# Moving SBUF tiles to other addresses: weights at 0 and moving tiles at 64 modulo 256 bytes, in an attention, FFT and feed-forward kernel

## The chip, the core and the metric

The kernel runs on one core of a Trainium2 chip. The metric is the device time of one execution in microseconds. The profile of one execution names the engines PE (TensorE's matmuls), PEld (TensorE's weight loads), DVE (VectorE), ACT (ScalarE), POOL (GpSimd) and SP (SyncE, which issues most DMAs). A matmul has two operands in SBUF: the stationary one, which a weight load brings into the array, and the moving one, which is streamed past it.

## What is computed

Cut from the reference: four batches, 12 heads, 448 tokens, head size 64, so 768 features; the feed-forward layer is 3072 wide.

```python
scores = cap * np.tanh(scale * np.matmul(q, k.transpose(0, 1, 3, 2)) / cap)
attn = np.exp(scores - np.max(scores, axis=-1, keepdims=True))
attn = attn / (np.sum(attn, axis=-1, keepdims=True) + 1e-09)
x = np.matmul(attn, v)                       # then to (batch, token, 768)
u = x + np.real(np.fft.fft(np.fft.fft(x, axis=1), axis=2))
un = (u - mean(u)) / np.sqrt(var(u) + 1e-06)
out = u + np.maximum(un @ w_ch1, 0.0) @ w_ch2
```

## The kernel before

The work has two stages that overlap a little. In the **attention stage** (to about 195 us) 84 steps run: `scores` (L398) multiplies k tiles (stationary) with q tiles (moving) in fp32, ACT takes tanh (L408) and exp (L411) into tiles `a`, and `weigh` (L427) multiplies `a` (stationary) with `vt` (moving, 65 columns). Batch by batch the FFT follows as small matmuls with constant tables (L499, L527), and the residual stream is transposed (L611).

The **feed-forward stage** (from about 200 us to the end) is in 12 rounds `g`, each of 256 of the 3072 hidden features. `up` (L737 to L758) makes, for one batch, two PSUM tiles `ph` of 18 matmuls each: six feature blocks `dc`, and for each three products, low weights with high x, high weights with low x, high with high (L744), since every fp32 number is split in two fp32r parts. Relu goes to `hh` (ACT L756 the high part, DVE L757 the low part). `down` (L760 to L792) makes six PSUM tiles `po` of 6 matmuls each, two `hh` tiles by the same three products, and DVE adds each to the residual `xc` (L787). Every matmul of both lines has 128 rows and 448 moving columns of 4 bytes, except the last group of all, which is cut into 256 and 192 columns. One round is `U0 U1 D0 U2 D1 U3 D2 D3` (L796; U is up, D is down, the digit is the batch): 36 matmuls for each letter, 288 in a round. In round 0 the order is `U0 D0 U1 D1 U2 D2 U3 D3`.

The weights come as 64-bit numbers in `raw` tiles by DMA (two buffers of tag `raw` for the first rounds, two of tag `seq` later) and are split into two fp32r parts by six or seven DVE instructions and two of ACT for each half tile (`jobs`, L634 to L695); in the feed-forward stage DVE does this for the next round while PE works on this one. The order of all steps is a written table (`ORDER`) and a fixed interleaving after it; nothing in it depends on addresses.

SBUF is handed out by `new()` (L299): all tiles of the stages come from one pool, under a tag with a number of buffers; a pool lays out its tags one behind the other. A tile of more than 100 elements is rounded up to `LINE` = 16 elements (64 bytes). Several kinds of tiles share a tag one after the other. The weights of round `g` for `up` are in tag `w1` when g is even and in tag `x0` when g is odd (`PLACE1`, L75); those for `down` take `w2a`, `w2b` and two `raw` buffers in turn (`PLACE2`, L76). The moving x operands `xs` of batch 0, 1, 2, 3 are in tags listed in `XPLACE` (L84): batches 0 and 1 in tiles that all begin at 64 modulo 256 bytes, batch 3 in `ff`, `y` and `feat`, of which five of six begin at 0. `hh` shares the five `a` buffers (L755).

Of the kernel before, what the change touches and what calls it, by code (L numbers as in the profile page):

```python
# [11 lines left out]
F32 = mybir.dt.float32  # L12
# [7 lines left out]
P = 128  # L20
# [38 lines left out]
GF = 2  # L59


LINE = 16


HI_MIN = float(np.uint32(0x38100000).view(np.float32))
# [209 lines left out]
def attention_fft_ffn(  # L275
# [12 lines left out]
    nc = tc.nc  # L288
    add, sub, mul = ALU.add, ALU.subtract, ALU.mult
    keep = ctx.enter_context(tc.tile_pool(name="keep", bufs=1))  # L290
    dram = ctx.enter_context(tc.tile_pool(name="dram", bufs=4, space=bass.MemoryType.DRAM))


    pool = ctx.enter_context(tc.tile_pool(name="pool", bufs=1))
    psum = ctx.enter_context(tc.tile_pool(name="psum", bufs=2, space=PSUM))
    stage = {}
    turn = {}

    def new(shape, dtype, tag, bufs, name):  # L299
        n = math.prod(shape[1:])  # L300
        flat = pool.tile([P, -(-n // LINE) * LINE if n > 100 else n], dtype, tag=tag, bufs=bufs, name=name)
        axes = [f"d{i}" for i in range(len(shape) - 1)]
        sizes = {a: z for a, z in zip(axes[1:], shape[2:])}
        return flat[: shape[0], :n].rearrange(f"p ({' '.join(axes)}) -> p {' '.join(axes)}", **sizes)

    def turns(shape, dtype, tags, bufs, name):
        turn[name] = n = turn.get(name, -1) + 1
        return new(shape, dtype, tags[n % len(tags)], bufs, name)
# [10 lines left out]
    ident = keep.tile([P, P], F32, name="ident")  # L319
    make_identity(nc, ident)  # L320
    capt, tscale, ncap, guard = (keep.tile([P, 1], F32, name=n) for n in ("capt", "tscale", "ncap", "guard"))
    mhalf = keep.tile([P, LINE], F32, name="mhalf")
    nc.vector.memset(mhalf, -0.5)
    nc.scalar.activation(guard, mhalf[:, :1], AF.Tanh)

# [3 lines left out]


    vt = new([P, 2, NC, D + 1], F32, "vt", 1, "vt")
    nc.gpsimd.memset(vt[:, :, :, D:], 1.0)

# [23 lines left out]
    def load_constant(i):  # L357
        n, p = divmod(i, 2)
        if p == 0:
            featT[n] = new([P, 2, S], F32, "feat", 2, "featT")  # L360
            nc.sync.dma_start(featT[n][:, :, :NJ], feat[n])
        else:
            seqT[n] = new([P, 2, NK], F32, "seq", 2, "seqT")
            nc.sync.dma_start(seqT[n], seq[n])
# [93 lines left out]
    t_t, f_t, y_t, u_t, d_t, stat, line, lnrow, rowt = ({} for _ in range(9))  # L458
# [553 lines left out]
```

## Time and profile before

| | us |
|---|---|
| median of the runs | 922.57 |
| quickest run | 922.36 |
| the profiled execution, its own time | 923.11 |
| its span, first to last instruction | 921.3 |
| PE busy in it | 908.7 |
| DVE busy | 716.6 |
| ACT busy | 327.9 |

The span is 1.8 us shorter than the execution's own time. PE's busy time counts a matmul from its start to a modelled end; the matmuls overlap, so the pace, from one start to the next, is to be taken from long stretches of equal instructions and not from the mean duration of one. The chain of waits lists, in order of time, what each stretch of the execution waited for; a row "14.40 PE ph L745 x72" is 72 matmuls in a row which took 14.40 us together.

### The profile page before, as it was taken

To read this page: it belongs to the slowest core of one execution; us is meant where nothing else is said; L and a number is where in the kernel's file an instruction comes from. 1 tells how busy PE (TensorE), PEld (TensorE's weight loads), DVE (VectorE), ACT (ScalarE), POOL (GpSimd) and SP (SyncE) were. 2 spreads that over 40 slices of the span, in tenths; PEclk is the share of its full clock that TensorE was granted. 3 is DMA by queue.
4 is the path that set the end of the run, shared out by engine and by line. 5 is a ranking of instruction groups with operands and counts; after the bars stand their busy time and mean duration, and the time that the engine had idled before them with its cause. 6 is when DMAs were issued, how large, how long until landed. Compare 5 with 4: busy or idle time off the path is not lost.

```text
span 921.3 us, 18681 instructions
## 1 busy us (share of the span) xinstructions
PE 908.7 (99%) x7836; PEld 790.8 (86%) x7836; DVE 716.6 (78%) x1467; ACT 327.9 (36%) x503; POOL 6.8 (1%) x15
## 2 busy tenths in 40 slices
PE   8999999999999999999999999999999999999998
PEld 5676766677889999999999999999999999999997
DVE  2688797999988787887878778787787877877633
ACT  7998889962412222122121222212222221222200
POOL 0000000000000000000000000000000000000000
PEclk9999999999999999999999999999999999999999
DMA  6654433400202221211212111111211112121033
GB/s 184 185 169 129 117 91 96 123 15 2 80 20 67 56 75 52 62 52 52 64 53 71 58 51 52 52 52 54 67 52 52 52 51 54 55 64 52 18 120 120
DMA packets 50612, 66.64 MB, mean 72 GB/s; under 512 B 25568, under 2 KB 36704, under 8 KB 50528
## 3 DMA queue, kind: packets, MB, share of 16 engines
q1 hardware_dynamic: 50240, 65.12, 24.7%
q8 instruction: 62, 1.02, 0.5%
q10 hardware_dynamic: 288, 0.33, 0.1%
q14 instruction: 22, 0.18, 0.1%
HBM read 59.91 MB, written 5.52 MB: 71 GB/s over the span
## 4 chain that ended last, share of the span: by engine, by line
PE 92%; DVE 3%; ACT 3%; issue 1%; DMA 1%; POOL 0%; SPq 0%; DVEq 0%; POOLq 0%; ACTq 0%
PE po L779 38%; PE ph L745 37%; PE av L427 7%; PE s L398 6%; PE pq L527 1%; PE yps L499 1%; ACT a L408 1%; ACT a L411 1%; PE pt L611 1%; DMA capt<-cap 1%; DVE u L551 0%; ACT u L602 0%; ACT hh L756 0%; DVE u L547 0%; DVE u L604 0%
## 5 line engine op out<-in xcount | busy, mean ns | idle before, releaser
L779 PE MATMUL po<-hh,w 128*128 128x448 f32 x1734 | 361.4, 366 | 1.7 <-DVE xc L787 1.3
L745 PE MATMUL ph<-xs,w 128*128 128x448 f32 x1728 | 356.5, 365 | 0.0
L779 PEld LDWEIGHTS po<-hh,w 128*128 128x128 f32 x1734 | 323.2, 188 | 32.7 <-DVE xc L787 4.7
L745 PEld LDWEIGHTS ph<-xs,w 128*128 128x128 f32 x1728 | 324.0, 188 | 25.6 <-issue 0.3
L787 DVE TENSOR_TENSOR xc<-xc,po 128x448 f32<-128x448 f32 x289 | 176.3, 615 | 41.4 <-PE po L779 41.1
L757 DVE SCALAR_TENSOR_TENSOR hh<-ph,hh 128x448 fp32r<-128x448 f32 x96 | 59.9, 624 | 95.8 <-ACT hh L756 95.6
L658 ACT ACTIVATE wt<-raw 128x384 f32<-128x384 f32 x84 | 46.5, 554 | 230.4 <-DVE w L692 230.4
L756 ACT ACTIVATE hh<-ph 128x448 fp32r<-128x448 f32 x96 | 52.4, 545 | 189.6 <-PE ph L745 189.6
L427 PEld LDWEIGHTS av<-vt,a 128*49 128x49 f32 (+3 forms) x3072 | 85.1, 130 | 28.4 <-issue 14.6
L427 PE MATMUL av<-vt,a 128*49 128x65 f32 (+3 forms) x3072 | 91.2, 222 | 1.5 <-issue 1.0
L408 ACT ACTIVATE a<-s,tscale 128x900 f32<-128x900 f32 x84 | 82.7, 1009 | 13.0 <-PE s L398 8.5
L411 ACT ACTIVATE a<-a,capt 128x900 f32<-128x900 f32 x84 | 85.7, 1047 | 0.9
L312 ACT CAST w<-wt 128x384 fp32r<-128x384 f32 x84 | 42.8, 509 | 117.7 <-DVE wt L667 117.7
L398 PE MATMUL s<-q,k 64*64 64x450 f32 x672 | 76.4, 552 | 1.8 <-ACT a L408 1.7
L667 DVE SCALAR_TENSOR_TENSOR wt<-wt 128x384 f32<-128x384 f32 x96 | 53.6, 558 | 9.6 <-DVE wt L664 0.5
L664 DVE SCALAR_TENSOR_TENSOR wt<-raw,wt 128x384 uint32<-128x384 uint32 x96 | 53.6, 559 | 3.3
L692 DVE TENSOR_TENSOR w<-wt 128x384 fp32r<-128x384 f32 x96 | 53.6, 558 | 3.3
L686 DVE SCALAR_TENSOR_TENSOR wt<-raw,wt 128x384 f32<-128x384 uint32 x96 | 53.5, 558 | 2.9
L317 DVE TENSOR_TENSOR wt<-wt,w 128x384 f32<-128x384 f32 x96 | 52.8, 550 | 0.0
L398 PEld LDWEIGHTS s<-q,k 64*64 64x64 f32 x672 | 19.9, 132 | 21.8 <-ACT a L408 10.3
L661 DVE TENSOR_SCALAR wt<-raw 128x384 uint32<-128x384 uint32 x96 | 34.1, 355 | 1.1
L683 DVE TENSOR_SCALAR wt<-wt 128x384 uint32<-128x384 uint32 x96 | 34.0, 354 | 0.6
(59 smaller groups left out, 326.1 us busy)
## 6 DMA issues: line engine op xcount, KB each, us to landing
raw<-w2r SPq DMA_DIRECT2D x48, 384.0 KB, 3.1
raw<-w1r SPq DMA_DIRECT2D x48, 384.0 KB, 3.1
q<-qr SPq DMA_DIRECT2D x35, 225.0 KB, 3.3
outT<-xc SPq DMA_DIRECT2D x23, 224.0 KB, 1.9
k<-kr SPq DMA_DIRECT2D x12, 256.0 KB, 3.2
vt<-vr SPq DMA_DIRECT2D x24, 128.0 KB, 4.3
vt<-vr SPq DMA_DIRECT2D x24, 96.0 KB, 2.5
k<-kr SPq DMA_DIRECT2D x12, 192.0 KB, 3.4
```

Source lines behind the costliest of these rows:

```text
L398: nc.tensor.matmul(ps_t[t][h * D : (h + 1) * D, n, :SQ], kt[q, k][rows, k0, h], qk[q, x][rows], start=True, stop=True,)
L408: nc.scalar.activation(a_t[t], ps_t.pop(t)[:, :, :SQ], AF.Tanh, scale=tscale)
L411: nc.scalar.activation(a_t[t], a_t[t], AF.Exp, scale=capt)
L427: nc.tensor.matmul(pa_t[p][q0:q1, j, g * (D + 1) : (g + 1) * (D + 1)], a_t[t][rows, n, OFF[g] + q0 : OFF[g] + q1], vt[rows, p % 2, i], sta ...
L664: nc.vector.scalar_tensor_tensor(tu, hi.bitcast(U32), 0xC0000000, tu, op0=ALU.bitwise_and, op1=ALU.bitwise_or)
L667: nc.vector.scalar_tensor_tensor(t, w, HI_MIN, t, op0=ALU.is_ge, op1=mul)
L686: nc.vector.scalar_tensor_tensor(w, lo, 2.0**-52, w, op0=mul, op1=mul)
L692: nc.vector.tensor_tensor(ws[c][1][:, sl], t, w, op=add)
L745: nc.tensor.matmul(ph[:, :S], w_[:, dc * P : (dc + 1) * P], x_, start=(k_ == 0), stop=(k_ == 3 * NDC - 1),)
L757: nc.vector.scalar_tensor_tensor(hh[:, 1], ph[:, :S], 0.0, f32(hh[:, 0]), op0=ALU.max, op1=sub)
L779: nc.tensor.matmul(po[:, q0:q1], w_[:, dc * P : (dc + 1) * P], hh[:, x_, q0:q1], start=(k_ == 0), stop=(k_ == 3 * GF - 1),)
L787: nc.vector.tensor_tensor(ac[:, q0:q1], ac[:, q0:q1], po[:, q0:q1], op=add)
```

## The change

The one pool is cut into three: small tiles first, then a pool of everything that is loaded as weights of the feed-forward stage and what shares its tags, then all other large tiles. Two pad tiles shift where the second and third pool begin, and `LINE` goes from 16 to 64 elements (256 bytes), so that every tile in a pool begins at the same place modulo 256 bytes. The room for it comes from small tiles that are no longer rounded up and from a descriptor scratch of 1 KB in place of 16 KB a partition, which shifts all of SBUF down.

```diff
-LINE = 16
+LINE = 64
+WEIGHTS = "w1", "x0", "w2a", "w2b", "raw", "seq", "tmp"
+SMALL = "den", "stat", "bs", "ln", "nt", "var", "rowt", "yh"
+PAD = 16, 16
...
-    pool = ctx.enter_context(tc.tile_pool(name="pool", bufs=1))
+    pools = {2: ctx.enter_context(tc.tile_pool(name="small", bufs=1))}
+    pad = ctx.enter_context(tc.tile_pool(name="pad", bufs=1))
+    pad.tile([P, PAD[0]], F32, name="pad")
+    pools[1] = ctx.enter_context(tc.tile_pool(name="weights", bufs=1))
+    gap = ctx.enter_context(tc.tile_pool(name="gap", bufs=1))
+    gap.tile([P, PAD[1]], F32, name="gap")
+    pools[0] = ctx.enter_context(tc.tile_pool(name="pool", bufs=1))
...
-        flat = pool.tile([P, -(-n // LINE) * LINE if n > 100 else n], dtype, tag=tag, bufs=bufs, name=name)
+        home = pools[1 if tag in WEIGHTS else 2 if tag in SMALL else 0]
+        size = n if tag in SMALL else -(-n // LINE) * LINE
+        flat = home.tile([P, size], dtype, tag=tag, bufs=bufs, name=name)
...
-    mhalf = keep.tile([P, LINE], F32, name="mhalf")
+    mhalf = keep.tile([P, 4], F32, name="mhalf")
...
-    nc = bacc.Bacc("TRN2", target_bir_lowering=False, num_devices=1)
+    nc = bacc.Bacc("TRN2", target_bir_lowering=False, num_devices=1, dynamic_dma_scratch_size=1024)
```

Every engine's list of instructions, with their shapes and the semaphores they wait for, is the same in both built programs, but for one memset of `mhalf` that is 4 columns wide in place of 16. What differs is addresses. The built programs give each operand's first byte in its partition; modulo 256 it is:

| operand | before | after |
|---|---|---|
| `up` weights, even g / odd g | 0 / 192 | 0 / 0 |
| `up` moving `xs`, batches 0 and 1 | 64 | 64 |
| `up` moving `xs`, batch 2 | 0, 64, 128, 192 | 64 |
| `up` moving `xs`, batch 3 | 0 (15 of 18 matmuls), 64 (3) | 64 |
| `down` weights | 192 (1155 matmuls), 0 (579) | 0 |
| `down` moving `hh`, by buffer | 128, 192, 0, 64, 128 | 64 |
| `scores` moving q, by buffer / stationary k | 128, 192, 0, 64 / 128 | 64 / 64 |
| `weigh` tile `a` by buffer / `vt` | 128, 192, 0, 64, 128 / 64 | 64 / 64 |

An offset inside a weight tile (512 bytes for a block `dc`, 3072 from the high to the low part) and from the high to the low half of a moving tile (1792 bytes) is a whole number of 256 bytes, so it changes nothing in this table. Of the 3462 matmuls of `up` and `down`, those with moving minus weights equal to 64 modulo 256 are 792 of 1728 and 330 of 1734 before, and all of them after.

## Rows read from the trace of the kernel before

**Rows 1.** The page: busy time of the engines, and the chain that ended last

```profile
PE 908.7 (99%) x7836; PEld 790.8 (86%) x7836; DVE 716.6 (78%) x1467; ACT 327.9 (36%) x503; POOL 6.8 (1%) x15
...
PE po L779 38%; PE ph L745 37%; PE av L427 7%; PE s L398 6%; PE pq L527 1%; PE yps L499 1%; ACT a L408 1%; ACT a L411 1%; PE pt L611 1%; DMA capt<-cap 1%; DVE u L551 0%; ACT u L602 0%; ACT hh L756 0%; DVE u L547 0%; DVE u L604 0%
```

**Rows 2.** Busy time by stretch: PE, PEld, DVE, ACT, POOL, then PEclk, DMA share, GB/s

```profile
300.00:350.00 50.00, 50.00 (x249) 46.51 (x248) 39.73 (x78) 11.15 (x22) 0.00 (x0) 1.00 0.21 59
```

**Rows 3.** The page's costliest groups: the two matmul lines

```profile
L779 PE MATMUL po<-hh,w 128*128 128x448 f32 x1734 | 361.4, 366 | 1.7 <-DVE xc L787 1.3
L745 PE MATMUL ph<-xs,w 128*128 128x448 f32 x1728 | 356.5, 365 | 0.0
```

**Rows 4.** Chain of waits, U0 and U1 of g=1, 2 and 4: start, us, what

```profile
274.17 14.69 PE ph L745 x72
...
332.57 14.40 PE ph L745 x72
...
449.94 14.41 PE ph L745 x72
```

**Rows 5.** Chain of waits, U3 of g=1, 2 and 8

```profile
310.68 7.24 PE ph L745 x36
...
369.16 7.29 PE ph L745 x36
...
720.79 7.39 PE ph L745 x36
```

**Rows 6.** Chain of waits, the whole round g=10 and the start of g=11

```profile
801.17 14.40 PE ph L745 x72
815.57 7.31 PE po L779 x36
822.88 7.36 PE ph L745 x36
830.23 7.32 PE po L779 x36
837.55 7.29 PE ph L745 x36
844.84 14.65 PE po L779 x72
859.49 14.69 PE ph L745 x72
```

**Rows 7.** Chain of waits: D1 of g=2, D2 with D3 of g=4, D0 of g=8

```profile
361.60 7.56 PE po L779 x36
...
493.88 14.93 PE po L779 x72
...
698.87 7.27 PE po L779 x36
```

**Rows 8.** Chain of waits, around the start of the last unbroken stretch of PE

```profile
268.46 0.54 DVE xc L787
...
269.05 5.12 PE po L779 x24
```

**Rows 9.** Chain of waits, its end

```profile
918.07 0.02 issue
```

**Rows 10.** Waits of PEld from 265 us on: total us, times, longest

```profile
PEld po L779 <- DVE xc L787: 2.8, 9, 0.5
```

**Rows 11.** Timeline of PE in the attention stage: start, us, and what

```profile
29.99 1.89 PE L398 MATMUL s<-q,k 64*64 64x450 f32 x16
31.70 2.18 PE L427 MATMUL av<-vt,a 64*64 64x65 f32 x80
...
36.27 1.74 PE L398 MATMUL s<-q,k 64*64 64x450 f32 x16
...
103.16 2.55 PE L427 MATMUL av<-vt,a 128*64 128x65 f32 x80
```

**Rows 12.** A DVE line that reads `raw` tiles: duration ns min/median/max

```profile
L664 DVE SCALAR_TENSOR_TENSOR wt<-raw,wt x96: 557/559/561, 10.5 to 865.9; 128x384 uint32<-128x384 uint32 x96
```

## The prediction

> **What bounds the kernel now.** I read the page first: PE is busy for 908.7 us of the span, and its two feed-forward lines hold 38% and 37% of the chain that ended last, the attention lines 7% and 6% [rows 1]. So what counts is how fast PE gets through its matmuls. [...]
>
> The groups by line cannot show the pace, since their matmuls overlap: 365 and 366 ns is the mean length of one, and both lines have the same form, 128x448 [rows 3]. The chain in order of time can, because it merges unbroken rows of equal matmuls. There the reader is to see two things.
>
> First, the pace is not constant although the work is. U0 and U1 of each round are 72 matmuls of one form on the same x tiles (all at 64 modulo 256). They took 14.69 us in g=1, 14.40 in g=2, 14.41 in g=4 [rows 4]. The eleven rounds after the first alternate strictly: six odd ones took 14.68 or 14.69 us, five even ones 14.40 or 14.41. What alternates with them is one thing, the place of the `up` weights: 192 modulo 256 when g is odd, 0 when it is even. That is 204.0 against 200.1 ns a matmul.
>
> Second, it is the distance between the operands that counts, not the weights' place by itself. Batch 3 has nearly all its x tiles at 0, and there the order turns round: U3 took 7.24 us in g=1, with the weights at 192, and 7.29 and 7.39 in g=2 and 8, with the weights at 0 [rows 5]. The good cases are 64 minus 0 and 0 minus 192, both 64 modulo 256; the worse ones are 128 and 0. So while a matmul streams its moving operand and the next weights are loaded, the two reads seem to hinder each other by an amount that their relative place sets. The trace shows the effect, not its mechanism.
>
> Of the whole stretch from 269.05 us, where the chain leaves DVE [rows 8], to 918.07 us [rows 9] the chain is PE without a break: 649.02 us. In it lie 24 matmuls of round 0 and eleven rounds of 288 (the last six, cut in two, count as six), 3192 in all: 203.3 ns each.
>
> **The change part by part.** *Up.* After the change all 1728 matmuls of `up` have the operands of the 14.40 us rows, 64 and 0. 936 of them have another distance now. *Down.* All 1734 of `down` get the same; 1404 have another distance now. Before, weights, `hh` tiles or both change place in the middle of each group of six, and one kind of `down` row is at distance 64 in both halves, but at different places (64 and 0, then 0 and 192): D0 of g=8, 7.27 us for 36 [rows 7], 201.9 ns. The clean round g=10 shows where `down` stands otherwise: 7.31, 7.32 and 14.65 us for 36, 36 and 72 [rows 6], 203.1 to 203.5 ns. After, nothing changes place within a group or from one group to the next, as within U0 and U1 of an even round, and the form and the sequence of low and high parts are the same. So I carry 200.1 ns over from `up`, and keep 201.9 as the other bound.
>
> The sum: at 14.405 us for 72 a matmul takes 200.1 ns, 3192 take 638.7 us, and 649.02 - 638.7 is 10.3 us. Not all of this is pace. In g=2 to 5 PE also waits: D1 took 7.56 us in g=2 [rows 7] against 7.32 in the clean round, 0.24 more, and so in four rounds, 1.0 us; D2 with D3 took up to 14.93 us [rows 7] against 14.65, about 0.6 us over the four. These 1.6 us are waits of the weight load for DVE's addition to the residual, which frees the PSUM tile [rows 10], and no address changes them. That leaves 8.7 us.
>
> Two corrections. Before 269 us the chain runs through DVE and ACT between short pieces of PE [rows 8]: this transition, with the last batch's FFT, sets its own time. Round 0 has 264 matmuls there; at 3.2 ns each (203.3 - 200.1) they could give 0.8 us, and nothing if all is hidden. I take 0.3, since most of that stretch is the other engines'. Then a faster PE meets the four waiting rounds earlier, where DVE is late already, and part of the gain turns into longer waits. If DVE alone set those four rounds, all the gain of the pace in them would be lost: a clean round is 58.32 us from start to start [rows 6] and 288 times 200.1 ns is 57.63, so 0.7 us a round, 2.8 us in four. If DVE follows, nothing is lost. DVE has 10 of 50 us free there [rows 2] and its additions follow PE's groups, so I stay near nothing and take 0.5 of the 0 to 2.8 us. Sum: 8.7 + 0.3 - 0.5 = **8.5 us**.
>
> *Attention.* Its operands move too: q and k come to the same place (64 and 64), `a` and `vt` as well. Before, q goes round four buffers at all four places and `a` round five, so a strong effect would show as steps of several lengths in turn. They don't: of the six unbroken pairs of steps in the two stretches that I read, one took 1.89 us and the rest 1.74 or a little less [rows 11]. A run of 80 `weigh` matmuls took 2.18 or 2.55 us [rows 11], which goes with its shapes. So I price the stage at nothing. If the share of long pairs went from one in six to none, 42 pairs would gain 0.025 us each, 1.0 us; if it went to one in two, they would lose 0.05 each, 2.1 us.
>
> *DVE, ACT, DMA.* Nothing is added or moved in any queue: no instruction, no wait. A DVE line that reads `raw` tiles at 192 early and at 0 later took 557 to 561 ns throughout [rows 12], so I see no price of an address there. The wider rows make no operand longer. The memset of 4 in place of 16 columns stands before the first matmul and costs nothing.
>
> The profiled execution took 923.11 us, its span 921.3; less 8.5 it would be 914.6. The median of the runs is 0.54 lower, and so is the forecast: 922.57 - 8.5 = **914.1 us**, 0.9% faster. By about 2% a measurement of this kernel tells a change from none, so this counts as the same.
>
> [...] The even and odd rows above differ by 0.28 us with nothing but an address changed [rows 4]. [...]
>
> **The rivals.** *Addresses make no difference*, and the alternation has another cause that also goes by odd and even rounds, such as which weights DVE and the DMAs write meanwhile. Then the time stays at 922.6 us. Against it stands that U3 turns the other way from U0 and U1 in the same rounds [rows 4, 5]; for it, that U3's order rests on 0.05 to 0.15 us. That the tiles don't lie where the change says is no rival: the built program gives 64 and 0 for every matmul of both lines.
>
> *Only `up` gains.* In `down` each group of six begins with a new PSUM tile, whose release and whose `hh` PE may have to wait for, and it might not settle in the quick pattern. Then the gain is `up`'s alone: in g=10 14.40 + 7.36 + 7.29 [rows 6] against 144 times 200.1 ns, 28.81, so 0.24 us; in an odd round 0.28 from the first two batches and 0.04 each from the others at 7.24; about 0.3 in eleven rounds, 3.3 us: 919.3 us. For it speaks that `down` is slower than `up` in mixed rounds. *`Down` gains in part*, as its own row at distance 64 would have it: 1.8 ns more for the 1596 matmuls of `down` in the stretch, 2.9 us, and 917.0 us.
>
> *DVE takes it back.* The four waiting rounds keep their length, and 2.8 us are lost in place of 0.5: 922.6 - 6.2 is 916.4 us. For it speaks that PE's waits in them are all for DVE [rows 10], against it that they sum to 2.8 us in nine waits, so DVE is late by little.
>
> *Attention slows* and the kernel ends slower than before. Its stationary and moving operands now begin at the same place, distance 0, which in U3 is the worse case. If all pieces went from the quick to the slow row, scores would cost 84 times 0.075 us (half of 1.89 - 1.74), 6.3 us, and `weigh` 3072 times 4.6 ns ((2.55 - 2.18) / 80), 14.2 us [rows 11]. The pieces are mixed now, so I take half, 10.3 us: 922.6 - 8.5 + 10.3 = 924.4 us. It ends slower from 8.5 us on, 4.4% of the stage's 195 us. Against it: q and `a` pass through that distance already in part of the steps.
>
> **How the numbers follow.** The forecast has a chance of 0.68 (from 911.5, if the transition gives its 0.8, nothing goes to DVE, attention gives its 1.0 and the 0.6 of waits at D2 and D3 go: 8.7 + 0.8 + 1.0 + 0.6 = 11.1; to 916.2, if attention loses its 2.1), `down` gaining in part 0.13, DVE taking it back 0.05, only `up` 0.06, no difference 0.05, attention 0.03. The range must leave out no more than 0.2: no difference and attention are beyond it, half of only `up`, and some of the forecast's own case where two of its ends meet. It goes from 911.5 to 919.2 us, the upper end just at only `up`. Faster by over 2% would need 904.1 us, a pace of 197.5 ns (18.5 us off 649.02), which no row of 72 shows: 0.01. Slower by over 2% is 941: 0.02, for a mishap in attention at its full 20.5 us and more. The rest is 0.97.
>
> **What would show it.** In the chain after the change, every U0 with U1 should read about 14.41 us in odd rounds too, every U2 and U3 7.20, a clean D0 7.20 to 7.24, and a round 57.6 to 57.8 us from start to start. The first 195 us should end where they do now, within 2 us. The waits of PEld for DVE may grow from 2.8 us [rows 10], by no more than 2.8. If a clean D0 stays at 7.27 or above, the carrying over from `up` to `down` was wrong; if the odd rounds stay at 14.69, the whole reading was; if the start of the last unbroken stretch of PE moves from 269 us by more than 2, the attention or the transition does depend on addresses.

## The result

The changed kernel takes 914.82 us (median of 6 runs, 913.74 to 915.91) against 922.57 us for the kernel before (median of five, 922.25 to 923.82), a ratio of 0.9913 with a 95% interval of 0.9899 to 0.9926: 7.8 us by these medians, 8.0 us by the ratio, 0.9% faster. A sixth execution of the kernel before took 1494.82 us and is left out. By the 2% that separates a change from none it counts as the same. The forecast was 914.1 us in a range of 911.5 to 919.2. The profiled execution took 914.81 us, with a span of 913.0 us and a mean granted clock of 0.999.

The chain of waits of the changed kernel, in order of time (start us, us, what), answers to [rows 4 to 9]; g=1, parts of g=2, 4 and 10, and the start of g=11 are shown.

```profile
268.44 5.07 PE po L791 x24
273.52 14.40 PE ph L757 x72
287.92 7.20 PE po L791 x36
295.12 7.20 PE ph L757 x36
302.32 7.20 PE po L791 x36
309.52 7.20 PE ph L757 x36
316.72 14.40 PE po L791 x72
...
359.92 2.40 PE po L791 x12
362.32 0.02 issue
362.34 5.08 PE po L791 x24
367.42 7.20 PE ph L757 x36
374.62 14.63 PE po L791 x72
...
490.87 7.21 PE po L791 x36
498.07 0.05 issue
498.13 7.57 PE po L791 x36
...
794.29 14.40 PE ph L757 x72
...
851.90 14.40 PE ph L757 x72
...
909.64 0.02 issue
```

Three things are to be seen. Every clean piece, of `up` and of `down`, of odd and of even rounds, is 7.20 or 7.21 us for 36 matmuls, or twice that for 72: 200.0 ns for one matmul, or little more. The even-odd pattern of [rows 4] and the opposite pattern of U3 [rows 5] are gone. The clean round g=10 takes 57.61 us (851.90 - 794.29) against 58.32 [rows 6]. And the waits stay in the same places: D1 of g=2 is cut in two at 362.32 and takes 7.50 us with the gap, D2 and D3 14.63 us, and 14.83 in g=4.

The unbroken stretch of PE now runs from 268.44 to 909.64 us, 641.20 us for the same 3192 matmuls, against 649.02 [rows 8, 9]: 7.8 us of the 8.3 that the span lost. It begins 0.6 us earlier. PE's waits for DVE's additions [rows 10] read, for the weight loads from 264 us on,

```profile
PEld po L791 <- DVE xc L799: 3.0, 9, 0.5
```

so they grew by little. The attention stage is the same: a run of 80 `weigh` matmuls takes 2.55 us and a pair of steps 1.74 us, as in [rows 11], and the last exp starts at 192.4 us (192.6 before).

### The profile page after: what moved, and what is told of

Same layout as the page of the kernel before. It is cut to its first block, busy times and chain, and to the rows that moved or that the text cites. A ratio compares the mean times of both kernels' runs of the same rounds, so it can differ in the third digit from the quotient of the medians.

```text
span 913.0 us, 18681 instructions
## 1 busy us (share of the span) xinstructions
PE 901.6 (99%) x7836; PEld 789.7 (86%) x7836; DVE 715.9 (78%) x1467; ACT 327.9 (36%) x503; POOL 6.8 (1%) x15
## 4 chain that ended last, share of the span: by engine, by line
PE 91%; DVE 4%; ACT 3%; issue 1%; POOL 0%; DVEq 0%; POOLq 0%; ACTq 0%
PE po L791 37%; PE ph L757 37%; PE av L439 7%; PE s L410 6%; PE pq L539 1%; ACT a L423 1%; ACT a L420 1%; PE yps L511 1%; PE pt L623 1%; DVE u L559 0%; DVE u L563 0%; ACT u L614 0%; PE warm L349 0%; DVE tf L480 0%; DVE xc L747 0%
## 5 line engine op out<-in xcount | busy, mean ns | idle before, releaser
L791 PE MATMUL po<-hh,w 128*128 128x448 f32 x1734 | 356.9, 363 | 1.8 <-DVE xc L799 1.3
L757 PE MATMUL ph<-xs,w 128*128 128x448 f32 x1728 | 352.5, 362 | 0.0
L799 DVE TENSOR_TENSOR xc<-xc,po 128x448 f32<-128x448 f32 x289 | 176.3, 615 | 38.3 <-PE po L791 38.1
```

The lines of the kernel that those rows point to most:

```text
L757: nc.tensor.matmul(ph[:, :S], w_[:, dc * P : (dc + 1) * P], x_, start=(k_ == 0), stop=(k_ == 3 * NDC - 1),)
L791: nc.tensor.matmul(po[:, q0:q1], w_[:, dc * P : (dc + 1) * P], hh[:, x_, q0:q1], start=(k_ == 0), stop=(k_ == 3 * GF - 1),)
L799: nc.vector.tensor_tensor(ac[:, q0:q1], ac[:, q0:q1], po[:, q0:q1], op=add)
```

## Experiments

**The theories.** The prediction's theory: the pace of PE is set by the distance of the moving operand from the weights modulo 256 bytes, and 64 is a good one. The rivals: it is the absolute place of the weights (0 is good); or only that all tiles are alike or rounded up; or addresses play no part. Four kernels change nothing but the two pad tiles.

```diff
-PAD = 16, 16    # distance 64, weights at 0
+PAD = 16, 32    # d128:    weights at 0,  moving tiles at 128
+PAD = 16, 64    # d0:      weights at 0,  moving tiles at 0
+PAD = 16, 48    # d192:    weights at 0,  moving tiles at 192
+PAD = 32, 16    # shift64: weights at 64, moving tiles at 128
```

> Weights at 0, moving tiles at 128 modulo 256 (second pad tile 32 elements wide in place of 16), distance 128. If the distance between the operands sets the pace, every U0 with U1 reads 14.69 us, as the odd rounds of before did, a round 58.7 to 59.0 us, and the time is 914.8 + 3192 x 3.9 ns = 927.3 us. If only the place of the weights counts (0 is good), or only that all tiles are alike or padded, 914.8 us and 14.40. If addresses make no difference and something else in the change gained the 8 us, 914.8 us.

> Weights at 0, moving tiles at 0 modulo 256 (second pad tile 64 wide), distance 0. By the distance theory about 204 to 206 ns a matmul (batch 3 of before, nearly all at distance 0 in even rounds, took 7.29 to 7.39 us for 36), U0 with U1 14.7 to 14.8 us, time 927 to 934 us, slower than the kernel before. By the theory that the weights' place at 0 or equal tiles made the gain, 14.40 and 914.8 us.

> Weights at 0, moving tiles at 192 modulo 256 (second pad tile 48 wide), distance 192. The trace of before has this distance only in mixed groups of down, at 201 to 205 ns. By the distance theory about 202.5 ns, U0 with U1 14.58 us, time 922.8 us (919 to 927). By the others 14.40 and 914.8 us.

> Both pools moved on by 64 bytes (first pad tile 32 wide): weights at 64, moving tiles at 128 modulo 256, distance 64 as in the changed kernel. By the distance theory nothing changes: U0 with U1 14.40 us, 914.8 us. If the absolute places count (weights at 0, or moving at 64), the pace falls back to that of mixed rounds or worse: 14.6 us or more, 922 to 928 us.

Measured, as ratio to the kernel before on the same chip, with its interval:

| run | distance | U0 with U1, us | median us | ratio |
|---|---|---|---|---|
| d0 | 0 | 14.59 or 14.88 | 930.20 | 1.0084 (1.0056 to 1.0111) |
| the changed kernel | 64 | 14.40 | 914.82 | 0.9913 (0.9899 to 0.9926) |
| shift64 | 64 | 14.40 | 914.87 | 0.9909 (0.9894 to 0.9923) |
| d128 | 128 | 14.69 | 926.88 | 1.0036 (1.0021 to 1.0050) |
| d192 | 192 | 14.56 | 922.13 | 0.9987 (0.9977 to 0.9996) |

The lengths of U0 with U1 are those of the one profiled execution of each kernel. For d0 that was its slowest, 934.86 us; the other three took 929.64 to 930.53.

The same program in the same order is 12.1 us slower with the moving tiles 64 bytes further on, and loses nothing when the weights move with them. In the chains, one round's first piece reads, for d128, d0 (two rounds), d192 and shift64:

```profile
569.20 14.69 PE ph L757 x72
```

```profile
512.91 14.60 PE ph L757 x72
...
571.78 14.88 PE ph L757 x72
```

```profile
567.04 14.56 PE ph L757 x72
```

```profile
563.98 14.40 PE ph L757 x72
```

d128 was worked out as 914.8 + 3192 x 3.9 ns = 927.3 us and measured at 926.88. All rivals expected 914.8 in d128, d0 and d192, or 922 and more in shift64; they fall. That the distance between the moving tiles and the weights is the cause is shown. The granted clock has no part in it: its mean over the profiled execution is 1.000 in d128, d192 and shift64 alike and 0.999 in the changed kernel. Only that of d0 is lower, 0.996, and the other three executions of d0 had 1.000 and took 929.64 us at the least. Nor have DVE and ACT as they write the weight tiles: in d128 the last such instruction of DVE starts at 873.0 us, and the pieces behind it are as slow as those before it:

```profile
884.99 7.34 PE ph L757 x36
```

**Is 64 an optimum, and how sharp?** Two kernels stand 32 bytes beside it.

```diff
+PAD = 16, 8     # d32: moving tiles at 32
+PAD = 16, 24    # d96: moving tiles at 96
```

> Weights at 0, moving tiles at 32 modulo 256 (second pad tile 8 wide), distance 32. If the pace is a smooth function of the distance between 0 (206.6 or 202.7 ns) and 64 (200.0), U0 with U1 reads 14.5 to 14.7 us and the time is 917 to 925 us. If 64 is no optimum but the pace has a floor of about 200 over a range of distances, 14.40 and 914.8 us. If the pace goes by steps of 64 bytes, it is that of distance 0: 14.6 to 14.9, 923 to 935 us.

> Weights at 0, moving tiles at 96 modulo 256 (second pad tile 24 wide), distance 96. Smooth between 64 (200.0 ns) and 128 (204.0): 14.5 to 14.6 us for U0 with U1, 919 to 923 us. Floor around 64: 14.40, 914.8 us. Steps of 64 bytes: as distance 64, 14.40, 914.8 us. An optimum above 64 would read under 14.40.

Both are slower than the kernel before: d32 932.48 us, ratio 1.0109 (1.0092 to 1.0125), d96 931.38 us, ratio 1.0087 (1.0072 to 1.0102). d96 reads 14.78 us, worse than 64 and worse than 128, so neither the smooth course, nor a floor, nor steps of 64 bytes fit: every one of the three guesses is wrong for it.

```profile
571.39 14.78 PE ph L757 x72
```

d32 is stranger. Its U0 with U1 of g=2 to 8, and D2 with D3 of g=7 before the last of them:

```profile
333.66 14.72 PE ph L757 x72
392.43 14.40 PE ph L757 x72
451.03 14.88 PE ph L757 x72
510.80 14.88 PE ph L757 x72
570.23 14.40 PE ph L757 x72
627.84 14.40 PE ph L757 x72
...
671.04 14.52 PE po L791 x72
685.55 14.72 PE ph L757 x72
```

One program, one distance, three paces: 200.0, 204.4 and 206.7 ns. It falls into one of them and keeps it: in g=2 to 5 until D1 or D2, where PE waits for DVE, and after 685.55 us to the end. The change inside the 14.52 us piece of g=7 has no wait beside it in the profile. Its runs differ, from 926.46 us (the profiled one) to 934.20; that they differ by these paces is likely, but no other was profiled. d0 has two such paces, 14.59 and 14.88, and changes between them only in g=2 to 5, at D1 or D2. So the distance does not set the pace outright; it seems to set which steady patterns are possible, and of the six distances 64 was the only one at which PE ran at 200.0 ns throughout.

**One part alone.** In wonly the weights stand at 0 in a pool of their own, the moving tiles are rounded to 64 bytes as before.

```diff
-        size = n if tag in SMALL else -(-n // LINE) * LINE
+        line = LINE if tag in WEIGHTS else 16
+        size = n if tag in SMALL or n <= 100 else -(-n // line) * line
```

> One part of the change alone: the weights in their own pool at 0, but the moving tiles rounded to 64 bytes as before, so they begin at 0, 64, 128 and 192. U0 and U1 have distance 64 throughout, the others mixed ones (down: 345 matmuls at 64, 684 at 128, 342 at 192, 363 at 0). If the distance sets the pace, U0 with U1 reads 14.40 us in all rounds, D1 to D3 7.30 or more for 36, and with 204.1, 202.3 and about 204.7 ns for 128, 192 and 0 the sum is 7.1 us over the changed kernel: 921.9 us. If the weights' place alone makes the gain, 914.8 us.

It took 921.20 us, ratio 0.9980 (0.9970 to 0.9989); 921.9 was worked out from the paces of the other runs. U0 and U1, at distance 64, are quick, the rest is not:

```profile
566.96 14.40 PE ph L758 x72
581.36 7.33 PE po L792 x36
588.69 7.30 PE ph L758 x36
```

Fixing the weights alone gives 1.8 of the 8.0 us (by the ratios); the rest comes only with the moving tiles. The moving tiles alone were not tried.

**Which pair of operands?** A matmul's own moving operand and weights, or its moving operand and the weights that are loaded beside it for the next one (from 564 to 910 us of the changed kernel PE is busy for 345.62 us and PEld, at the same time, for 323.60): in the kernel all of these have one distance. Two kernels part them in U0 and U1 of g=1 to 11, which are interleaved matmul by matmul.

```diff
+        for pair in (((0, 0), (1, 1)), ((1, 0), (0, 1))):   # (batch, half of the weights)
...
+                for wi, xi in ((1, 0), (0, 1), (0, 0)):
+                    for (b, n), p_ in zip(pair, ph):
+                        nc.tensor.matmul(
+                            p_[:, :S],
+                            w1s[GF * g + n][wi][:, dc * P : (dc + 1) * P],
+                            xs[b, dc][xi],
...
+SHIFT = 16      # cross: batch 1's x and the weights' second half 64 bytes further on
+SHIFT = 32      # cross128: 128 bytes further on
```

> Which pair of operands counts: a matmul's own, or its moving operand and the weights that are loaded beside it for the next one? The changed kernel, but U0 and U1 of g=1 to 11 are interleaved matmul by matmul, and batch 1's x tiles and the second half of the round's up weights stand 64 bytes further on. In the first 36, a matmul has its own distance 64 (64 and 0, 128 and 64 in turn), and the load beside it has distance 0 or 128; in the second 36 it is the other way round. If the load beside the stream counts, the first 36 take 7.34 to 7.40 us and the second 7.20. If a matmul's own pair counts, 7.20 and then 7.34 to 7.40. If neither, both 7.20. U2 and U3 have 64 and 0 by halves, about 7.27 to 7.32 each. Time 918 to 920 us in either of the first two cases.

> The interleaved U0 and U1 again, with batch 1's x tiles and the second half of the round's up weights 128 bytes further on in place of 64, so that each half is of one kind: in the first 36 every matmul's own distance is 64 and the load beside it has 192, in the second 36 the own distance is 192 and the load beside it has 64. All at 64 took 7.20 us for 36, all at 192 took 7.28. If a matmul's own pair sets the pace, 7.20 then 7.28; if the load beside the stream does, 7.28 then 7.20; if both count, neither half reads 7.20 or both read something between. The time stays near 930 us, since D0 waits for the two hidden tiles that now end together.

cross took 930.99 us, ratio 1.0088 (1.0073 to 1.0103), and cross128 930.39 us in its one run, the 930 expected of it. The 918 to 920 us expected of cross left out that D0 now waits for two hidden tiles that end together. In the chain of cross, 1.9 us of ACT and DVE stand behind the interleaved piece; four of D0's 36 matmuls run meanwhile, so PE loses about 1.2 us of it in a round (D0 takes 8.4 us from its first start to the next piece, and 7.20 without a wait):

```profile
586.02 0.55 ACT hh L797
...
586.60 1.17 DVE hh L798 x2
...
587.81 6.67 PE po L820 x32
```

The halves are what counts. In cross the first half of g=8 and the second (the chain cut to each) read 7.00 us for 35, the quick pattern, and 7.31 for 36; in g=3 it was 7.12 for 35 and 7.32 for 36. The first half is quick in six of the eleven rounds and at 203.3 ns in five, by the starts of the matmuls; the second is never quick.

```profile
689.87 7.00 PE ph L785 x35
```

```profile
696.87 7.31 PE ph L785 x36
```

In cross128 the two halves of the same round read 7.06 and 7.13 us for 35, which is 201.7 and 203.7 ns; in g=9 they read 7.06 for 35 and 7.27 for 36, 201.7 and 201.9 ns. All eleven rounds are like one of these two. The first and second half of g=8:

```profile
689.10 7.06 PE ph L785 x35
```

```profile
696.36 7.13 PE ph L785 x35
```

In none of these halves does cross128 reach 200.0 ns, although in each of them one of the two pairs has distance 64. That is the third outcome: both pairs count, or at least neither alone sets the pace. cross agrees for its second halves, where the load beside is at 64 and the own pair is not; its first halves do not decide, since with its own distance at 64 a half can be quick, and was not in every round. That 200.0 ns was reached there shows at least that the interleaving by itself does not stop it. Whether a third pair counts, such as a moving tile and the weights two matmuls on, was not tried.

**What the waits are, and what they cost.** The prediction left 1.6 us of waits in place and gave 0.5 us of the gain to longer ones. In nores the additions of the means in g=2 to 5 are gone (the four lines of the two conditions); in spread, whose diff follows, they stand in other places.

```diff
-        b, k_ = i // (12 * B) - 2, i % (12 * B)
-        if b in range(B) and k_ == 0:
-            later(row, b, 0)
-        if b in range(B) and k_ % 8 == 7:
-            later(residual, b, k_ // 8, 0)
+        r, k_ = i // (12 * B) - 2, i % (12 * B)
+        if r in range(2 * B) and r % 2 == 0 and k_ == 0:
+            later(row, r // 2, 0)
+        if r in range(2 * B) and k_ in (7, 15, 31):
+            later(residual, r // 2, r % 2 * 3 + (7, 15, 31).index(k_), 0)
```

> The changed kernel without the second addition to the residual: rounds g=2 to 5 no longer load and add the row of means (row and residual with n=0 are left out, so the output lacks that term). The waits of PE that remain in the feed-forward stage lie in just these four rounds. If they come from those additions on DVE, standing ahead of the one that frees a PSUM tile, D1 of g=2 to 5 reads 7.20 and D2 with D3 14.41, all rounds 57.62 us, and the time is 914.8 - 2.2 = 912.6 us. If they come from the conversion of the weights, they stay: 914.8 us.

> The changed kernel with the additions of the means spread over g=2 to 9, three a round in place of six, at pieces 7, 15 and 31 of a round, where the changed kernel shows no wait behind them (they were at 7, 15, 23, 31, 39, 47). Nothing is left out. If the waits come from additions that stand right ahead of D1's and D2's first groups, they go: 57.62 us a round, 912.6 us. If any addition costs its 0.61 us of DVE wherever it stands, the waits are spread too and the time stays at 914.8 us.

> The kernel before, all addresses as they were, with the additions of the means spread over g=2 to 9 as in the run spread. It tells what the waits cost before the change: in the changed kernel they cost 2.6 us (914.8 to 912.2). If the quicker PE turned part of its gain into longer waits on DVE, the waits cost less here, 1.6 us as summed in the prediction: 921.4 us. If they cost the same, the change lost nothing to them: 920.4 us.

nores took 912.28 us, ratio 0.9881 (0.9866 to 0.9895), spread 912.16 us, ratio 0.9885 (0.9870 to 0.9901): the 912.6 expected, and the same for both, though spread does all of the additions. In spread, D1 of g=2 and D2 with D3 read

```profile
359.26 7.20 PE po L791 x36
366.46 7.20 PE ph L757 x36
373.66 14.42 PE po L791 x72
```

So the waits come from where the additions stand, right ahead of the first additions of D1 and of D2 that free the PSUM tile, and not from DVE's whole load, which is the same. The timeline of the changed kernel shows one in D1 of g=2: the addition of a mean (L747), then the one that frees the tile (L799), then the weight load that had waited 0.39 us:

```profile
361.14 0.62 DVE L747 TENSOR_TENSOR xc<-xc,mean 128x448 f32<-128x448 f32 x1
361.67 0.61 DVE L799 TENSOR_TENSOR xc<-xc,po 128x448 f32<-128x448 f32 x1
...
362.34 0.71 PEld L791 LDWEIGHTS po<-hh,w 128*128 128x128 f32 x4 [0.39 <-DVE xc L799]
```

spread has three additions a round where there were six, so place and number in a round are not told apart by the times. That the weights' conversion alone made the waits falls. By its median spread is quicker than both kernels.

bspread, the kernel before with the additions spread, took 920.80 us, ratio 0.9978 (0.9969 to 0.9987). The waits thus cost 2.0 us before the change (1.2 to 2.9) by this ratio, and 2.6 after it by the ratios of spread and the changed kernel. That the quicker PE made them longer agrees with the sign, but the intervals overlap; the times don't settle it. The chains do better. Piece by piece against bspread, the four D1 of before lose 0.25 us each and the four D2 with D3 0.1 to 0.35, 1.8 us together (the 1.6 of the prediction took g=10 for all rounds); against spread, those of the changed kernel lose 0.3 each and 0.2 to 0.4, 2.25 us. So they grew by some 0.45 us.

## Why the prediction was right

*The reading.* That the alternation of 14.69 and 14.40 us [rows 4] with only the place of the weights changed, and its reversal in U3 [rows 5], meant the distance of the operands, is shown by shift64 against d128, d0 and d192. The rival without addresses would have needed 922.6 us.

*The pace in `up` and its carrying over to `down`.* 200.1 ns was forecast for all 3192 matmuls, 200.0 measured in every clean piece of both. The other bound, 201.9 ns from D0 of g=8 [rows 7], was the wrong neighbour: there the tiles changed place within each group, so a matmul beside such a change streams against a load at distance 128 or 0. That this made the 1.9 ns more fits cross128, but no run isolates it. (The 1596 matmuls that the prediction gives to `down` in the stretch are 1608; its 2.9 us stay.)

*The sum.* 8.7 us in the long stretch, less 0.5 to longer waits, was 8.2; measured 7.8. The waits were 1.8 us and not 1.6, and grew by 0.45, near the 0.5 that was set down with little to go by. The rest is mainly the first and the last piece: the 24 matmuls at 268.44 us take 5.07 us and not 4.80, and the last 72, of which six are cut in two, 14.54 and not 14.40; the pace itself was 0.1 ns better than forecast. The transition gave 0.6 us, inside its 0 to 0.8; I had taken 0.3. Together 8.5 was forecast and 7.8 (by the ratio 8.0, by the spans 8.3) measured.

*The rivals.* DVE taking back 2.8 us did not come; spread shows that a few places in DVE's order, not its whole load, make the waits. Attention is where it was, to 0.2 us. By the built programs all matmuls of `scores` have distance 0 now, and about a fifth of them had it before; `weigh` takes slices of `a` that begin at many places, so its matmuls have mixed distances before and after, although the tiles begin alike. So no loss was seen for the small f32 matmuls of `scores` at distance 0; for `weigh` no run tells anything.

*The sign that was not seen.* I took the pace for a function of the distance. d32 and d0 show several paces at one distance. The forecast did not depend on it, since distance 64 was in the trace of before in an unbroken form, in U0 and U1 of five rounds; at a distance that was not, the same reasoning would have failed, as it did for d96. That distance 64 has no second, slower pattern, in `down` and behind each wait, was taken for granted, and in that the forecast had luck.

## What to carry to other kernels

Where a kernel is bound by matmuls that each load new weights, take the pace from unbroken pieces of the chain, not from mean durations, and look for equal pieces that differ: here such pieces differed by 2% (14.69 against 14.40 us) by their addresses alone, and one even-odd pattern gave the core of the prediction. Round tiles to 256 bytes and keep weights and moving operands in two pools, so that one constant can be tried at a few values; do not take a value that was not measured, since 32 bytes beside the best one cost 17 to 18 us by the medians. A wait that remains may be cured by moving a small instruction of another engine: additions of 0.6 us each, put elsewhere, gave 2.6 us.

## What was not expected of the hardware

The pace of 448-column fp32r matmuls with a weight load before each ran from 200.0 to 206.7 ns by operand addresses alone; the mean granted clock of these executions was 0.996 (d0), 0.998 (d32) and 0.999 or 1.000 (the others at one distance), a spread of 0.4% against 3.3% in the pace. At distances 0 and 32 the same program ran in two or three steady patterns, 202.6 and 206.7, or 200.0, 204.4 and 206.7 ns, and changed from one to another mostly where PE had waited, once without a wait in the profile. Why 64 bytes is good, and whether the two reads hinder each other, as the prediction supposed, no run here shows; distances other than multiples of 32, and 160 and 224, were not tried.
